# Three gate/up tiles leave the attention filler, the filler's order changes, and the sums of the input go to GpSimd

## The chip, the cores and the metric

The kernel runs on one core of one Trainium2 chip. The metric is device time in microseconds (us) of one execution, as the median of several runs; lower is better. The kernel before took 1116.48 us (median of 3, 1115.81 to 1116.67).

## The reference

One transformer block on x of 2048 tokens by 640, in float32. A layernorm without weights feeds two branches, and both are added to x:

```python
xn = _layernorm(x)                         # (x - mean) / sqrt(var + 1e-5)
# branch A: 32 heads of 20, causal, window of 256 tokens
q, k, v = split(xn @ wqkv)
scores = (q @ k^T) * 20 ** -0.5            # masked to 0 <= i - j < 256
o = softmax(scores) @ v
a = o @ wo                                 # 640 x 640
# branch B: gated MLP, 640 -> 1728 -> 640
g = xn @ w_gate ; u = xn @ w_up
b = (gelu_tanh(g) * u) @ w_down
out = x + a + b
```

## The kernel before

**Number format.** A dense product is made of three passes: each operand is split into a high and a low part of type fp32r, and high x high, low x high and high x low are added in PSUM (`dense_steps`, L78). With 640 = 5 x 128 inner rows, a 128 x 512 tile of output takes 15 matmuls, called steps here. The normalised input, transposed, stays in SBUF as `xh` and `xl`.

**Tiles of the MLP.** The 1728 columns of gate and up are 14 tiles f = 0 to 13 (the last one has 64 columns of each). A tile of gate and up for one of the four chunks of 512 tokens takes 2 x 15 = 30 steps, for all four chunks 120. The product gelu(g) * u is stored to DRAM (`hd`).

**Stages.** First a short stage does layernorm and transposes. Then comes attention (`attention`, L676), which takes more than half of the time. It runs over 32 units u (8 groups of 4 heads, times 4 chunks of tokens). Each unit is cut into NS = 14 slots, counted through the whole stage (slot 14u + i). The PE (TensorE) instructions of a unit are: matmuls for the maxima of the scores (`max_piece`, L410, 16 per unit, running one and a half units ahead), the scores again for the exponentials (`exp_piece`, L462, 12 per unit in three banks X, Y and Z, at slots 0 to 10), and in the next unit's first slot the product of P and v (`av_unit`, L484). DVE (VectorE) takes the maxima from PSUM (L412), ACT (ScalarE) the exponentials (L464), and POOL (GpSimd) zeroes the masked corners of P (`affine_select`, L470 and L473); `av_unit` needs all of a unit's selects.

**The filler.** Between these, `pull_fill` (L671) issues steps of dense work that attention does not need at once: RATE steps per unit, RATE / NS per slot. `filler` (L565) lists that work: q/k projections (`proj_qk`; q/k tile t of 10), v projections (`proj_v`), and gate/up tiles 0 to NFA - 1 and 13 (`gate_up_fill`, L520), in the order of the list `sets`. The second half of v is begun at the first turn after slot V1_SLOT. `gate_up_fill` makes the tanh form of gelu out of Square, Tanh and DVE operations (c1 to c5, each one slot after the other), since ACT also has to do Exp in this stage. A q/k projection is saved by `save_qk` (L196): ACT, DVE, ACT, and a subtraction on POOL (`pt`, L204), then stores on the SP queue. `load_stack` (L382) reads them back two units before they are used, six loads of 960 KB together.

**The seven-product phase.** After attention, tiles NFA to 12 are done by `gate_up_pair` (L833). It takes two chunks at once and uses seven block products in place of eight, over sums of weights (`w_sums`, on DVE) and sums of the input (`x_sums`, L602). A pair of chunks takes 54 matmuls, a tile 108, where the filler takes 120. Here gelu is one ACT operation. The sums of the input are made once, during attention: 8 groups (one per 50 slots from slot 24) of 10 operations on 128 x 256 elements, one per two slots, with four stores to DRAM (`td`, L616). They use two buffers `tx` in turn, so a new sum waits until the one two before has been stored.

**After that** the down projection and the output projection run (`terms`, L927), from 852 us to the end. The change touches nothing there.

**What sets the order.** In attention the orders on PE, ACT and DVE are written out by hand (`tc.manual_schedule(engines=MANUAL)`, with `defer` and `at` for slots). POOL and SP are not in that list: a planner puts their instructions into an order by times that it assumes, and each engine then executes its queue strictly in that order. The SP queue issues every DMA. In the seven-product phase SP is by hand too.

Of the kernel before, what the change touches and what calls it, by code (L numbers as in the profile page):

```python
# [12 lines left out]
AF = mybir.ActivationFunctionType  # L13
OP = mybir.AluOpType
# [10 lines left out]
NF = 14  # L25
# [2 lines left out]
NEG = -3.0e38  # L28
QROWS = 122
NS = 14  # L30
RATE = 49.6
V1_SLOT = 169
MXD = 4
NFA = 8
NDA = 2
WARM = 64
XS0, XSN = 24, 50
# [8 lines left out]
def block_kernel(ctx, tc, x, xt, wqk, wv, wo, wgu, wd, wdl, out):  # L46
    nc = tc.nc
# [30 lines left out]
    def dense_steps(ps, wh, wl, rh, rl, nk, cost=1.0):  # L78
        n = 0
        for a, b in ((wh, rh), (wl, rh), (wh, rl)):  # L80
            for k in range(nk):
                nc.tensor.matmul(ps, a(k), b(k), start=n == 0, stop=n == 3 * nk - 1)  # L82
                n += 1
                yield cost
# [89 lines left out]
    def defer(n, fn, *a):  # L174
        if now[0] is None:
            fn(*a)
        else:
            at(now[0] + n, fn, *a)
# [315 lines left out]
    def load_gu(f):  # L494
        raws = []
        for i in range(2 if f < NF - 1 else 1):
            raw = wrp.tile([128, KT, 128], F32, name="wr", tag="wr")
            nc.sync.dma_start(raw, wgu[2 * f + i])
            raws.append(raw)
        return raws  # L500
# [4 lines left out]
    def split_later(pool, bufs, raw):  # L505
        hi = pool.tile([128, KT, 128], F32R, name="wqh", tag="wqh", bufs=bufs)
        lo = pool.tile([128, KT, 128], F32R, name="wql", tag="wql", bufs=bufs)

        def high():
            nc.scalar.activation(hi, raw, AF.Copy)  # L510
            for k in range(KT):
                defer(1 + k, low, k)

        def low(k):
            nc.gpsimd.tensor_tensor(out=lo[:, k], in0=raw[:, k], in1=hi[:, k].bitcast(F32), op=OP.subtract)  # L515

        defer(1, high)
        return hi, lo

    def gate_up_fill(f, ws, c):  # L520
        cs = slice(c * C, (c + 1) * C)
        pss = []
        st = {}

        def c1():
            gs = st["g"] = hp.tile([128, C], F32, name="gs", tag="gs")
            t = st["t"] = hp.tile([128, C], F32, name="he", tag="he", bufs=2)
            nc.scalar.activation(gs, pss[0], AF.Copy)
            nc.scalar.activation(t, pss[0], AF.Square)
            defer(1, c2)  # L530

        def c2():
            gs, t = st["g"], st["t"]
            nc.vector.tensor_scalar(t, t, 0.044715, 1.0, op0=OP.mult, op1=OP.add)
            nc.vector.tensor_tensor(out=t, in0=gs, in1=t, op=OP.mult)
            defer(1, c3)

        def c3():
            nc.scalar.activation(st["t"], st["t"], AF.Tanh, scale=math.sqrt(2.0 / math.pi))
            defer(1, c4)  # L540

        def c4():
            nc.vector.scalar_tensor_tensor(st["g"], st["t"], 1.0, st["g"], op0=OP.add, op1=OP.mult)
            st["done"] = True

        def c5():
            if "done" not in st:
                defer(1, c5)
                return
            nc.vector.scalar_tensor_tensor(st["t"], st["g"], 0.5, pss[1], op0=OP.mult, op1=OP.mult)  # L550
            nc.sync.dma_start(hd[f][c], st["t"])

        for i, (wh, wl) in enumerate(ws):
            ps = psd.tile([128, C], F32, name="ps_d", tag="dn")
            pss.append(ps)
            yield from dense_steps(ps, lambda k: wh[:, k, :], lambda k: wl[:, k, :],
                                   lambda k: xh[:, k, cs], lambda k: xl[:, k, cs], KT)
            defer(1, c5 if i else c1)

    sets = [("qk", 1), ("gu", 0), ("qk", 2), ("gu", 1), ("qk", 3), ("gu", 2), ("qk", 4)]  # L560
    sets += [("gu", f) for f in range(3, NFA)] + [("gu", NF - 1)]
    pools = (wp, None), (hp, 2)
    rest = []

    def filler():  # L565
# [6 lines left out]
        for s, (kind, i) in enumerate(sets[:-1]):  # L572
            nxt = []
            after = sets[s + 1]
            for c in range(NC):
# [14 lines left out]
                if c in (1, 2) and c <= len(raws):  # L590
                    nxt.append(split_later(*pools[(s + 1) % 2], raws[c - 1]))
                if pending and now[0] >= V1_SLOT:
                    pending = False
# [8 lines left out]
    def x_sums(p, k, half):  # L602
        w = C // 2
        a, b = (slice((2 * p + i) * C + half * w, (2 * p + i) * C + half * w + w) for i in (0, 1))
        eh, el = xh.bitcast(F32), xl.bitcast(F32)
        live = {}

        def tile_of(i):
            live[i] = ap.tile([128, w], F32, name="tx", tag="tx")
            return live[i]  # L610

        def dve(o, i, j, op):
            nc.vector.tensor_tensor(out=o, in0=i, in1=j, op=op)

        def store(i):
            nc.sync.dma_start(td[p][i][:, k, half * w:half * w + w], live[i])  # L616

        def s1():
            dve(tile_of(1), eh[:, k, b], eh[:, k, a], OP.subtract)

        def s2():
            dve(live[1], live[1], el[:, k, b], OP.add)

        def s3():
            dve(live[1], live[1], el[:, k, a], OP.subtract)
            store(1)

        def s4():
            dve(tile_of(2), eh[:, k + 2, b], live[1], OP.subtract)

        def s5():
            dve(live[2], live[2], el[:, k + 2, b], OP.add)
            store(2)

        def s6():
            dve(tile_of(4), eh[:, k + 2, a], live[2], OP.subtract)

        def s7():
            dve(live[4], live[4], el[:, k + 2, a], OP.add)
            store(4)  # L640

        def s8():
            dve(tile_of(3), eh[:, k + 2, b], eh[:, k, b], OP.subtract)

        def s9():
            dve(live[3], live[3], el[:, k + 2, b], OP.add)

        def s10():
            dve(live[3], live[3], el[:, k, b], OP.subtract)
            store(3)  # L650

        return s1, s2, s3, s4, s5, s6, s7, s8, s9, s10

    NU = NG * NC
# [4 lines left out]
    def pull_max(n, slot):  # L659
        for _ in range(n):  # L660
            x = next(stream, None)
            if x is None:
                return
            max_piece(*x)
            if x[1] == 15:
                at(slot + MXD, max_end, x[0])
# [4 lines left out]
    def pull_fill(n):  # L671
        debt[0] += n
        while debt[0] > 0:
            debt[0] -= next(fill, 1.0)

    def attention():  # L676
# [15 lines left out]
        for u in range(NU + 1):  # L692
            if 1 <= u and u + 2 < NU:
                load_stack(u + 2)
            for i in range(NS):
# [5 lines left out]
                if i % 2 == 0:  # L701
# [3 lines left out]
                    pull_max(3 if i in (6, 12) else 2, T)  # L705
                pull_fill(RATE / NS)
        while acts:
# [77 lines left out]
    def load_xs(p, i):  # L785
        t = cp.tile([128, 2, C], F32, name="ht", tag="ht", bufs=3)
        nc.sync.dma_start(t, td[p][i])
        return t
# [167 lines left out]
    order.__enter__()  # L956
    raws_w = load_gu(NFA)
    xraw = {i: load_xs(0, i) for i in (2, 1, 3)}
# [61 lines left out]

    raws_next = {NFA + 1: load_gu(NFA + 1)}
    for j, f in enumerate(range(NFA, NF - 1)):
        end = f + 1 == NF - 1
# [56 lines left out]
    for n, (c, kind, i) in enumerate(steps):  # L1080
        if (kind, i) == ("d", 0):
            pss = [psn.tile([128, C], F32, name="ps_w", tag="w") for _ in range(KT)]
# [57 lines left out]
```

## Time and profile before

| | |
|---|---|
| median of 3 runs | 1116.48 us |
| profiled execution | 1116.69 us |
| its span in the profile | 1115.0 us |
| granted TensorE clock | 0.995 |
| busy share PE, DVE, ACT, POOL | 99%, 57%, 42%, 32% |

The profiled execution is 1.7 us longer than its span, and 0.2 us longer than the median. "Busy" for PE counts modelled ends of pipelined matmuls. A share of 99% thus says that little time is idle, not that each matmul is as short as it can be. The stages in the span: layernorm and start 0 to 92 us, attention 92 to 715 us, last gate/up tile 715 to 729 us, seven-product phase 729 to 852 us, down and output projection 852 to 1115 us.

### The profile page before, as it was taken

What the parts mean: (1) busy time and instruction counts of PE and PEld (TensorE: products, weight loads), DVE (VectorE), ACT (ScalarE), POOL (GpSimd) and SP (SyncE); (2) the same over time, 40 slices, a digit from 0 to 9 for tenths busy, and PEclk for the clock granted to TensorE, in tenths of its full rate; (3) what the DMA queues carried; (4) which work ended last, traced back from release to release, by engine and by line L of the source; (5) the groups of instructions that cost most, each with busy time, mean ns of one, the idle gap of its engine ahead of it and who ended that gap; (6) DMA issues with size and microseconds to landing.
All of it is one profiled execution on the core that took longest, in us unless ns stands there. A gap on an engine that the chain in (4) does not pass through costs nothing.

```text
span 1115.0 us, 19319 instructions
## 1 busy us (share of the span) xinstructions
PE 1098.7 (99%) x6802; PEld 837.6 (75%) x6802; DVE 637.7 (57%) x1736; ACT 470.9 (42%) x952; POOL 359.9 (32%) x504
## 2 busy tenths in 40 slices
PE   7999999999999999999999999999999999999998
PEld 7887666767668876667667676788888878788886
DVE  7856676757648577586777775566664350211203
ACT  4434554555555455645545454643323421211111
POOL 4122542644552233534323343311113313222230
PEclk8999999999999999999999999999999999999999
DMA  4642343543443314343242431342214835152431
GB/s 157 220 143 60 103 144 115 139 146 95 139 144 109 87 58 143 111 146 107 80 140 83 125 104 38 107 150 92 89 66 157 264 125 175 48 179 75 152 95 66
DMA packets 76145, 133.10 MB, mean 119 GB/s; under 512 B 12800, under 2 KB 33664, under 8 KB 76048
## 3 DMA queue, kind: packets, MB, share of 16 engines
q1 hardware_dynamic: 76048, 131.87, 37.6%
q8 instruction: 53, 0.87, 0.3%
q14 instruction: 44, 0.36, 0.1%
HBM read 86.31 MB, written 44.83 MB: 118 GB/s over the span
## 4 chain that ended last, share of the span: by engine, by line
PE 91%; DVE 4%; ACT 1%; DMA 1%; issue 1%; POOL 1%; SPq 0%; DVEq 0%; ACTq 0%; POOLq 0%
PE ps_d L82 28%; PE ps_w L942 23%; PE ps_g L851 11%; PE ps_o L484 7%; PE ps_e L462 7%; PE ps_m L410 6%; PE ps_v L82 6%; DVE junk L412 2%; PE ps_g L82 1%; PE ps_t L156 1%; PE ps_d L296 1%; ACT P L464 1%; PE ps_b L912 0%; DMA xi<-x 0%; DMA qs<-qd 0%
## 5 line engine op out<-in xcount | busy, mean ns | idle before, releaser
L412 DVE CUSTOM_DVE_ANT_0 junk<-ps_m,mask 128x384 bf16<-128x384 f32 (+2 forms) x512 | 271.2, 530 | 158.0 <-PE ps_m L410 120.0
L464 ACT ACTIVATE P<-ps_e 128x512 f32<-128x512 f32 (+2 forms) x384 | 197.5, 568 | 71.0 <-PE ps_e L462 64.6
L470 POOL TENSOR_SCALAR_AFFINE_SELECT P<-P 128x512 f32<-128x512 f32 x128 | 83.8, 655 | 221.1 <-ACT P L464 212.8
L82 PE MATMUL ps_d<-xh,wqh 128*128 128x512 f32 x510 | 150.4, 407 | 0.0
L82 PE MATMUL ps_d<-xh,wql 128*128 128x512 f32 x510 | 150.3, 407 | 0.0
L82 PE MATMUL ps_d<-xl,wqh 128*128 128x512 f32 x510 | 149.3, 406 | 0.0
L410 PE MATMUL ps_m<-ks,qs 120*128 120x128 bf16 (+1 forms) x704 | 120.9, 275 | 4.1 <-DVE mx L412 2.8
L921 POOL TENSOR_TENSOR ht<-hr,ht 128x512 fp32r<-128x512 f32 x52 | 69.2, 1337 | 172.1 <-ACT ht L919 142.9
L462 PE MATMUL ps_e<-qs,ks 122*128 122x128 bf16 (+2 forms) x704 | 112.5, 277 | 0.8 <-ACT P L464 0.6
L82 PEld LDWEIGHTS ps_d<-xl,wqh 128*128 128x128 f32 x510 | 92.9, 188 | 19.2 <-issue 2.4
L82 PEld LDWEIGHTS ps_d<-xh,wql 128*128 128x128 f32 x510 | 93.1, 189 | 18.0 <-issue 0.9
L82 PEld LDWEIGHTS ps_d<-xh,wqh 128*128 128x128 f32 x510 | 92.6, 188 | 17.2 <-ACT xh L164 0.3
L919 ACT ACTIVATE ht<-hr 128x512 fp32r<-128x512 f32 x56 | 35.1, 629 | 132.7 <-PE ps_w L942 80.8
L462 PEld LDWEIGHTS <-ks 122*128 122x128 bf16 x704 | 49.9, 98 | 54.6 <-issue 44.3
L473 POOL TENSOR_SCALAR_AFFINE_SELECT P<-P 128x512 f32<-128x512 f32 x112 | 74.2, 673 | 51.2 <-ACT P L464 51.2
L410 PEld LDWEIGHTS <-qs 120*128 120x128 bf16 x704 | 62.1, 98 | 33.1 <-issue 13.7
L484 PE MATMUL ps_o<-P,v 128*32 128x384 f32 (+2 forms) x1408 | 84.3, 386 | 0.0
L204 POOL TENSOR_TENSOR pt<-r,pt 128x512 bf16<-128x512 f32 x40 | 47.3, 1181 | 105.1 <-ACT pt L203 104.8
L484 PEld LDWEIGHTS ps_o<-P,v 128*32 128x32 f32 x1408 | 40.1, 110 | 39.6 <-issue 32.8
L923 DVE TENSOR_TENSOR ht<-hr,ht 64x512 fp32r<-64x512 f32 x4 | 2.8, 690 | 112.3 <-ACT ht L919 112.3
L515 POOL TENSOR_TENSOR wql<-wr,wqh 128x128 fp32r<-128x128 f32 x115 | 51.6, 481 | 38.0 <-ACT wqh L510 38.0
L488 ACT ACTIVATE ob<-ps_o 128x512 f32<-128x512 f32 x32 | 19.1, 597 | 101.1 <-PE ps_o L484 58.5
(270 smaller groups left out, 1889.2 us busy)
## 6 DMA issues: line engine op xcount, KB each, us to landing
hd<-he SPq DMA_DIRECT2D x52, 256.0 KB
hr<-hd SPq DMA_DIRECT2D x52, 256.0 KB
wr<-wgu SPq DMA_DIRECT2D x27, 320.0 KB
qs<-qd SPq DMA_DIRECT2D x32, 240.0 KB
ks<-kd SPq DMA_DIRECT2D x32, 240.0 KB
xi<-x SPq DMA_DIRECT2D x16, 320.0 KB
qs<-qd SPq DMA_DIRECT2D x32, 160.0 KB
ks<-kd SPq DMA_DIRECT2D x32, 160.0 KB
```

The lines of the kernel that those rows point to most:

```text
L82: nc.tensor.matmul(ps, a(k), b(k), start=n == 0, stop=n == 3 * nk - 1)
L410: nc.tensor.matmul(ps[:, lo:hi], lh, rhs, start=True, stop=True)
L412: nc.vector.tensor_tensor_reduce(out=junk[:, 0:n], in0=ps[:, 0:n], in1=mask[:, 384 - n:384], scale=1.0, scalar=NEG, op0=OP.add, op1=OP.max ...
L462: nc.tensor.matmul(ps[:, col:col + n], k[0:QROWS, j, kc:kc + 128], q[0:QROWS, j, q0:q0 + n], start=True, stop=True)
L464: nc.scalar.activation(pt[:, j, lo:hi], ps[:, lo:hi], AF.Exp, scale=SCALE)
L470: nc.gpsimd.affine_select(out=a, in_=a, pattern=[[0, 4], [1, 128]], compare_op=OP.is_ge, fill=0.0, base=0, channel_multiplier=-1)
L473: nc.gpsimd.affine_select(out=a, in_=a, pattern=[[0, 4], [-1, 128]], compare_op=OP.is_ge, fill=0.0, base=-1, channel_multiplier=1)
L484: nc.tensor.matmul(o[32 * j:32 * j + 32, q0:q0 + n], v[:, w0_:w0_ + 32], pt[:, j, col:col + n], start=i == 0, stop=i == len(todo) - 1, ski ...
L515: nc.gpsimd.tensor_tensor(out=lo[:, k], in0=raw[:, k], in1=hi[:, k].bitcast(F32), op=OP.subtract)
L851: nc.tensor.matmul(ps, i, j, start=first and n == 0, stop=n == len(work) - 1, skip_group_check=True)
L921: nc.gpsimd.tensor_tensor(out=t[:, 1, :], in0=raw, in1=t[:, 0, :].bitcast(F32), op=OP.subtract)
L942: nc.tensor.matmul(pss[m], w[:, ms], r, start=first and j == 0, stop=last and j == len(work) - 1)
```

## The change

- `NFA` goes from 8 to 5: tiles 5, 6 and 7 are no longer computed in the filler, but in the seven-product phase, which now has tiles 5 to 12 in place of 8 to 12.
- `RATE` goes from 49.6 to 38.4 steps per unit, so the smaller filler is spread over the same 32 units.
- `sets` is reordered: q/k tiles 1 and 2 first, then gate/up 0, q/k 3 and 4, then the other gate/up tiles.
- `V1_SLOT` goes from 169 to 174.
- The ten operations of each group of `x_sums` are issued on POOL in place of DVE. Their place on POOL's queue is up to the planner.
- In the filler's gelu, 0.044715 moves into the Square as a scale, and two DVE operations become one `scalar_tensor_tensor`.

```diff
-RATE = 49.6
-V1_SLOT = 169
+RATE = 38.4
+V1_SLOT = 174
...
-NFA = 8
+NFA = 5
...
-            nc.scalar.activation(t, pss[0], AF.Square)
+            nc.scalar.activation(t, pss[0], AF.Square, scale=math.sqrt(0.044715))
             defer(1, c2)
 
         def c2():
             gs, t = st["g"], st["t"]
-            nc.vector.tensor_scalar(t, t, 0.044715, 1.0, op0=OP.mult, op1=OP.add)
-            nc.vector.tensor_tensor(out=t, in0=gs, in1=t, op=OP.mult)
+            nc.vector.scalar_tensor_tensor(t, t, 1.0, gs, op0=OP.add, op1=OP.mult)
             defer(1, c3)
...
-    sets = [("qk", 1), ("gu", 0), ("qk", 2), ("gu", 1), ("qk", 3), ("gu", 2), ("qk", 4)]
-    sets += [("gu", f) for f in range(3, NFA)] + [("gu", NF - 1)]
+    sets = [("qk", 1), ("qk", 2), ("gu", 0), ("qk", 3), ("qk", 4)]
+    sets += [("gu", f) for f in range(1, NFA)] + [("gu", NF - 1)]
...
-        def dve(o, i, j, op):
-            nc.vector.tensor_tensor(out=o, in0=i, in1=j, op=op)
+        def pool(o, i, j, op):
+            nc.gpsimd.tensor_tensor(out=o, in0=i, in1=j, op=op)
...
         def s1():
-            dve(tile_of(1), eh[:, k, b], eh[:, k, a], OP.subtract)
+            pool(tile_of(1), eh[:, k, b], eh[:, k, a], OP.subtract)
...
```

The remaining lines of the diff replace `dve` by `pool` in s2 to s10 in the same way.

## The prediction

> **What bounds the kernel now.** First the page's busy shares, then the chain of work that ended last, then busy time by stretch.
>
> ```profile
> PE 1098.7 (99%) x6802; PEld 837.6 (75%) x6802; DVE 637.7 (57%) x1736; ACT 470.9 (42%) x952; POOL 359.9 (32%) x504
> ...
> PE 91%; DVE 4%; ACT 1%; DMA 1%; issue 1%; POOL 1%; SPq 0%; DVEq 0%; ACTq 0%; POOLq 0%
> PE ps_d L82 28%; PE ps_w L942 23%; PE ps_g L851 11%; PE ps_o L484 7%; PE ps_e L462 7%; PE ps_m L410 6%; PE ps_v L82 6%; DVE junk L412 2%; PE ps_g L82 1%; PE ps_t L156 1%; PE ps_d L296 1%; ACT P L464 1%; PE ps_b L912 0%; DMA xi<-x 0%; DMA qs<-qd 0%
> ```
>
> PE is the bound, and the chain is PE for 91%; the 2% of the maxima (L412) is where DVE is waited for. In the chain in order of time I read the attention units and the seven-product phase (start, length, count):
>
> ```profile
> 111.51 2.08 PE ps_o L484 x32
> 190.36 2.08 PE ps_o L484 x32
> 267.20 2.08 PE ps_o L484 x32
> 346.06 2.08 PE ps_o L484 x32
> 422.50 2.08 PE ps_o L484 x32
> 425.46 1.62 PE ps_d L82 x7
> 500.91 2.08 PE ps_o L484 x32
> 578.70 2.08 PE ps_o L484 x32
> 655.48 2.08 PE ps_o L484 x32
> 729.27 122.40 PE ps_g L851 x540
> ```
>
> Seven filler steps take 1.61 to 1.62 us: 0.230 us a step. The seven-product phase runs 540 matmuls without a break, 122.40 / 540 = 0.2267 us each. The x32 lines come once in four units: the fours last 78.85, 76.84, 78.86, 76.44, 78.41, 77.79 and 76.78 us, though PE's work differs little. Against the shortest, 8.9 us are lost to waits: mostly in fours with gelu and sums of the input together. By stretch (PE, PEld, DVE, ACT, POOL busy):
>
> ```profile
> 92.00:711.00 619.00, 614.09 (x4484) 438.28 (x4486) 419.20 (x1317) 328.23 (x674) 246.34 (x399) 1.00 0.36 110
> ...
> 778.23:802.71 24.48, 24.48 (x110) 20.27 (x109) 15.94 (x30) 7.07 (x15) 2.99 (x2) 1.00 0.23 79
> ```
>
> One tile of the seven-product phase takes 24.48 us with PE busy throughout, DVE at 65%. The groups that price the rest (mean ns of one):
>
> ```profile
> L921 POOL TENSOR_TENSOR ht<-hr,ht 128x512 fp32r<-128x512 f32 x52 | 69.2, 1337 | 172.1 <-ACT ht L919 142.9 <-DMA hr<-hd 29.1
> L515 POOL TENSOR_TENSOR wql<-wr,wqh 128x128 fp32r<-128x128 f32 x115 | 51.6, 481 | 38.0 <-ACT wqh L510 38.0
> L613 DVE TENSOR_TENSOR tx<-tx,xl 128x256 f32<-128x256 f32 x48 | 27.0, 564 | 0.0
> L535 DVE TENSOR_TENSOR he<-gs,he 128x512 f32<-128x512 f32 x32 | 24.0, 751 | 1.1
> L534 DVE TENSOR_SCALAR he<-he 128x512 f32<-128x512 f32 x32 | 14.7, 458 | 18.0 <-ACT he L529 17.8
> ```
>
> **The change part by part.**
>
> *Three tiles move.* The filler loses 3 x 120 = 360 steps x 0.230 = 82.9 us. The phase gains 3 x 24.48 = 73.4 us. Both are PE's path: **-9.5 us**. An added tile brings DVE 15.9, ACT 7.1 and POOL 3.0 us beside 24.48 us of PE; its two weight loads and eight stores lie in a DMA share of 0.23. All are hidden. Twelve filler gelus leave attention with their 1.8 us of ACT and 2.6 us of DVE each, as do 30 splits of 0.48 us on POOL: off the path by themselves.
>
> *Pace.* A unit loses 11.2 steps, 2.6 us: from 76.6 / 4 = 19.15 to some 16.55 us, a slot from 1.2 to 1.0 us. Attention's own work keeps its size, so every wait has less cover. DVE starts a maximum every 0.70 us in the timeline, 16 a unit: 11.2, and 0.3 for `nm`. Gelu then adds 14 slots / 11 per gelu = 1.28 x 3 operations of 0.7 = 2.7: 14.2 of 16.55, 86%. Before it was 15.8 of 19.15 (83%), and with sums (seven of 0.55 a unit where they run) 19.7, 103%. ACT's twelve exponentials at 0.55 us leave 0.9 us in each pair of slots of 2.0 us.
>
> *Sums off DVE, shorter gelu.* 80 sums (some 44 us) leave DVE, and L534 (0.46) goes from 20 gelus. The waits that this ends are in the 8.9 us: **-8.9**. What replaces them in gelu units is bounded by 0 (the four from 578.70, 0.3 us lost) and 0.6 us a unit (the worst fours, 2.4 us). I take 0.2, nearer the row at 83%, for 600 steps / 38.4 = 15.6 units: **+3.1** (0 to 9.4).
>
> *Sums on POOL.* No row has 256 columns there. Bounds are 0.48 (128 columns, L515) and 1.34 us (512, L921); between 0.48 and the 0.875 of the 320-column row (L239) it interpolates to 0.74, which I take. 80 x 0.74 = 59 us, less 14 for the splits, lift POOL from 40% to 53% of attention: not a bound. But POOL executes in order, and the planner's queue for the changed kernel puts the sums in clumps of up to five between the selects. Behind them stand the selects (`av_unit` waits), the q/k subtractions (L204), and on SP the stores of q/k with the loads of `load_stack` behind them. I follow POOL from a unit's start: selects of bank Y are ready at 10.1 and done at 12.0 us; those of Z are ready at 14.1, and PE wants Z at 16.6 + 1.8 = 18.4.
> Unit 7: five sums (3.7) and a weight split (2.4) stand between Y and Z: 18.1, and the first select ends at 18.7: 0.3 late.
> Unit 1: a split, a q/k subtraction (1.2) and four sums: 0.8 late.
> Unit 2: that lateness, one more sum and a subtraction end 4.4 us into it; three stores (1.3) and six loads (2.3 by the SP timeline) follow, and a load takes 3.88 us in the chain to land: 11.9, where the next stack's first maximum is due at 9.2: 2.7 late.
> Unit 11: v split, weight split and subtraction end 4.6 us into it: 2.9 late (before, that unit was already the longest, 20.43 us).
> Together **+6.7**; with sums of 0.48 or shorter waits it could be 0; with 1.34, 13.9.
> The `tx` stores now wait for POOL, but I find the maxima's rows (L427) queued behind them ready in time: with a slack of 1 us at units 11 and 13.
>
> *Order and V1_SLOT.* The q/k tiles now come with less filler work ahead of them. The second half of v starts at about slot 184 (the turn after V1_SLOT); at 9.75 / 2.74 = 3.6 slots per v tile its 16 tiles need 57 slots, and they are used over slots 238 to 294, the first four done by slot 198: hidden by some 40 slots of other work. Without that cover each late tile would cost its 9.75 steps, 2.2 us.
>
> Sum against the profiled execution: span 1115.0 - 9.5 - 8.9 + 3.1 + 6.7 = 1106.4, and 1.7 around it: **1108.1**; the median stands 0.2 below: **1108**.
>
> *A rule against it.* L613 has a median of 421 ns and a maximum of 1393, L535 starts 0.69 us apart when alone and has 1.00 beside POOL's work: DVE operations with both inputs in SBUF wait for POOL. The Trainium skill (SBUF - State Buffer, section Who interferes with whom) says that such an operation and a GpSimd instruction that reads SBUF take one port in turn, the second to issue blocking fully. The trace agrees; by that rule, two of gelu's three operations, blocked by a whole sum each, would make DVE's 14.2 us 16.1, just under 16.55, and by the rows' 0.2 to 0.3 us it is 15. The maxima (one input in PSUM) kept 0.56 us beside POOL's splits.
>
> **The rivals.**
> *A. Waits vanish.* The queues' slack is larger than I count (landing under 3.9 us): losses of 0 to 3 us, 1098.3 to 1101. For it: PE's recorded idle in attention is only 4.9 us.
> *B. The gain is eaten.* Sums of about 1.2 to 1.4 us (L921's length), or gelu units at 0.6 us: 1112 to 1117. Against it: L239 and L515 scale with columns.
> *C. Slower: POOL's sums delay the selects and stacks.* From 0.74 to 1.34 us the four places above lose 7.2 us more, 12 per us. The result is above 1118.7 once a sum takes 0.74 + 10.7 / 12 = 1.63 us, the length of 640 columns (L75, 1668 ns): 1119 to 1124. DVE's port waits speak for long sums, the 128-column row against.
> *D. DVE bounds gelu units.* By the port rule with waits on each gelu step: 16.1 to 17 us a unit, 0 to 0.5 us x 15.6: up to 1116. Against it: sums run in only 20 of 50 slots.
>
> **How the numbers follow.** Forecast 1102 to 1112: 0.57. A 0.13, B and D 0.18, C 0.12. A measurement tells 0.2% (2.2 us) from no change: faster is below 1114.2, slower above 1118.7. Faster: 0.57 + 0.13 + half of B and D = 0.79; same 0.09; slower 0.12. The bounds alone give 1098 to 1121; leaving out no more than 2 in 10, the range is 1101 to 1115.
>
> **What would show it.** The phase (L851) has 864 matmuls and about 196 us without a break; fours of units last about 66.5 us; L612 on POOL has 80 operations near 0.74 us; waits of L484 on POOL in units 1 and 7 and of L410 on loads in units 2 and 11. It is wrong if L484's waits on selects come in every unit, if L412 makes PE wait through whole gelu units, or if PE pauses between the phase's tiles.

## The result, and the profile after

The changed kernel takes **1126.05 us** (median of 4 runs, 1125.48 to 1126.12) beside 1116.58 us for the kernel before in the same session: a ratio of 1.0082 with a 95% interval of 1.0067 to 1.0097. It is slower by 0.8%, and 18 us above the 1108 us that were forecast. Its profiled execution took 1126.01 us with a span of 1124.3 us. All lines from L535 on have moved up by one against the kernel before.

The page's busy shares and its chain of work that ended last, by engine and by line:

```profile
PE 1097.3 (98%) x6766; PEld 832.2 (74%) x6766; DVE 610.0 (54%) x1657; ACT 467.6 (42%) x952; POOL 408.2 (36%) x560
...
PE 81%; DVE 6%; DMA 4%; issue 3%; ACT 3%; POOL 3%; SPq 1%; DVEq 0%; POOLq 0%; ACTq 0%
PE ps_w L941 19%; PE ps_d L82 18%; PE ps_g L850 17%; PE ps_o L484 7%; PE ps_m L410 6%; PE ps_e L462 5%; PE ps_v L82 5%; DVE junk L412 3%; DMA qs<-qd 2%; PE ps_g L82 1%; DMA od<-ob 1%; ACT P L464 1%; POOL ht L920 1%; PE ps_t L156 1%; POOL pt L204 1%
```

No engine but PE came near to being full: DVE fell from 57 to 54%, POOL rose from 32 to 36%. Yet PE's part of the chain went from 91 to 81%. Some of that is no loss: in the down and output projection the chain runs over PE for 222 of 264 us in place of 259 of 263, though PE waits for nothing there and the stage is as long as before, so there the chain only took another way. In attention PE's part went from 89% (552 of 623 us) to 74% (411 of 559 us), and what took its place is a bit of everything (DVE 46.5, DMA 33.2, ACT 26.0, POOL 19.1, "issue" 17.4 us). That is the picture of many short waits on several engines, and not of a new bound.

The chain in the order of time (start, length, count) says in which stage they lie:

```profile
110.06 2.17 PE ps_o L484 x32
182.10 2.08 PE ps_o L484 x32
251.22 2.08 PE ps_o L484 x32
326.16 2.16 PE ps_o L484 x32
394.38 2.08 PE ps_o L484 x32
463.35 2.08 PE ps_o L484 x32
531.50 2.08 PE ps_o L484 x32
...
650.88 13.89 PE ps_g L82 x60
664.78 195.85 PE ps_g L850 x864
```

The seven-product phase has its 864 matmuls in 195.85 us without a break, 73.45 us more than before, as forecast. From its end to the end of the span it is 263.7 us, against 263.3 before. So the error lies in attention: its last gate/up tile starts 64.5 us earlier than before (715.37 to 650.88), where the sum of the forecast wanted 82.0 (82.9 + 8.9 - 3.1 - 6.7). The fours of units last 72.0, 69.1, 74.9, 68.2, 69.0, 68.1 and 67.5 us, where about 66.5 were expected.

PE's waits in attention (90 to 651 us of the span; total, times, longest):

```profile
PE ps_m L410 <- DMA od<-ob: 6.1, 5, 2.5
PE ps_m L410 <- DVE mx L412: 5.6, 18, 0.4
PE ps_e L462 <- ACT P L464: 2.1, 5, 0.6
```

The first line is the loads of `load_stack`: the matmuls of L410 read only `ks` and `qs`, which these loads fill, and the profile puts the end of the wait down to a store (`od<-ob`) on the same queue. These 13.8 us were 4.3 us before (2.8 for maxima, 0.9 for transfers, 0.6 for exponentials). They are less than what was lost. One reason is that a wait is counted only from the modelled end of the last matmul: a filler step is recorded with 0.39 us, and the next one starts 0.23 us after it, so a stop is recorded some 0.16 us short. I therefore use another measure from here on: a unit's length less 0.2303 us for each filler step in it, the one that reaches over its start included (a 320-column step counted as 0.64 of one). What is left is the unit's own work. Unit n is here the stretch from the nth start of value products to the next. What is left is at its shortest about 7.33 us in one half of the units and 7.65 us in the other half, whose score matmuls are cut differently (7.31 and 7.63 in the kernel before, 7.35 and 7.78 in the changed one). What lies above 7.33 or 7.65 us, the same two figures in every run, I call the unit's **loss**. Summed over units 1 to 28, and split by what the changed kernel's filler mainly holds there:

```
loss, us              1-5   6-9   10-13  14-17  18-20  21-28   all
                      q/k   g/u   q/k    v      q/k    g/u
before                2.4   0.6    2.0   0.3    1.9    1.3     8.6
changed               6.0   3.5    8.9   2.0    2.6    3.2    26.1
forecast for changed                                           9.8
```

In the kernel before, q/k and gate/up work are mixed from unit 1 on, so its row stands for the same units and not for the same work. Two thirds of the changed kernel's loss, 17.5 of 26.1 us, lie in units whose filler is nearly all q/k work, with hardly a gelu. The forecast had charged the shorter pace to gelu's units alone.

### The profile page after: what moved, and what is told of

It reads as the page before. It is cut to its first block, busy times and chain, and to the rows that moved or that the text cites. A ratio compares the mean times of both kernels' runs of the same rounds, so it can differ in the third digit from the quotient of the medians.

```text
span 1124.3 us, 19237 instructions
## 1 busy us (share of the span) xinstructions
PE 1097.3 (98%) x6766; PEld 832.2 (74%) x6766; DVE 610.0 (54%) x1657; ACT 467.6 (42%) x952; POOL 408.2 (36%) x560
## 4 chain that ended last, share of the span: by engine, by line
PE 81%; DVE 6%; DMA 4%; issue 3%; ACT 3%; POOL 3%; SPq 1%; DVEq 0%; POOLq 0%; ACTq 0%
PE ps_w L941 19%; PE ps_d L82 18%; PE ps_g L850 17%; PE ps_o L484 7%; PE ps_m L410 6%; PE ps_e L462 5%; PE ps_v L82 5%; DVE junk L412 3%; DMA qs<-qd 2%; PE ps_g L82 1%; DMA od<-ob 1%; ACT P L464 1%; POOL ht L920 1%; PE ps_t L156 1%; POOL pt L204 1%
## 5 line engine op out<-in xcount | busy, mean ns | idle before, releaser
L412 DVE CUSTOM_DVE_ANT_0 junk<-ps_m,mask 128x384 bf16<-128x384 f32 (+2 forms) x512 | 271.8, 531 | 170.9 <-PE ps_m L410 128.4
L470 POOL TENSOR_SCALAR_AFFINE_SELECT P<-P 128x512 f32<-128x512 f32 x128 | 83.6, 653 | 176.6 <-ACT P L464 171.9
L410 PE MATMUL ps_m<-ks,qs 120*128 120x128 bf16 (+1 forms) x704 | 122.8, 275 | 11.9 <-DMA od<-ob 6.1
L920 POOL TENSOR_TENSOR ht<-hr,ht 128x512 fp32r<-128x512 f32 x52 | 69.1, 1333 | 172.6 <-ACT ht L918 152.7
L82 PE MATMUL ps_d<-xh,wqh 128*128 128x512 f32 x390 | 119.2, 412 | 0.0
L82 PE MATMUL ps_d<-xh,wql 128*128 128x512 f32 x390 | 118.8, 413 | 0.0
L82 PE MATMUL ps_d<-xl,wqh 128*128 128x512 f32 x390 | 118.4, 412 | 0.0
L462 PE MATMUL ps_e<-qs,ks 122*128 122x128 bf16 (+2 forms) x704 | 114.8, 278 | 3.3 <-ACT P L464 2.1
L410 PEld LDWEIGHTS <-qs 120*128 120x128 bf16 x704 | 61.9, 98 | 44.0 <-issue 20.7
L473 POOL TENSOR_SCALAR_AFFINE_SELECT P<-P 128x512 f32<-128x512 f32 x112 | 71.7, 651 | 26.5 <-ACT P L464 26.5
L82 PEld LDWEIGHTS ps_d<-xl,wqh 128*128 128x128 f32 x390 | 71.2, 190 | 13.6 <-issue 0.9
L82 PEld LDWEIGHTS ps_d<-xh,wql 128*128 128x128 f32 x390 | 70.8, 189 | 13.2 <-issue 1.1
L204 POOL TENSOR_TENSOR pt<-r,pt 128x512 bf16<-128x512 f32 x40 | 46.5, 1163 | 93.2 <-ACT pt L203 90.4
L82 PEld LDWEIGHTS ps_d<-xh,wqh 128*128 128x128 f32 x390 | 70.2, 189 | 13.2 <-issue 0.8
L75 POOL TENSOR_TENSOR wql<-wr,wqh 128x640 fp32r<-128x640 f32 x12 | 19.5, 1626 | 157.5 <-PE ps_g L850 127.6
L484 PEld LDWEIGHTS ps_o<-P,v 128*32 128x32 f32 x1408 | 40.1, 110 | 39.4 <-issue 28.4
L488 ACT ACTIVATE ob<-ps_o 128x512 f32<-128x512 f32 x32 | 19.1, 597 | 108.6 <-issue 60.0
```

What stands on the lines that cost most here:

```text
L204: nc.gpsimd.tensor_tensor(out=pt[:, l, :], in0=r, in1=pt[:, 1, :], op=OP.subtract)
L410: nc.tensor.matmul(ps[:, lo:hi], lh, rhs, start=True, stop=True)
L412: nc.vector.tensor_tensor_reduce(out=junk[:, 0:n], in0=ps[:, 0:n], in1=mask[:, 384 - n:384], scale=1.0, scalar=NEG, op0=OP.add, op1=OP.max ...
L462: nc.tensor.matmul(ps[:, col:col + n], k[0:QROWS, j, kc:kc + 128], q[0:QROWS, j, q0:q0 + n], start=True, stop=True)
L470: nc.gpsimd.affine_select(out=a, in_=a, pattern=[[0, 4], [1, 128]], compare_op=OP.is_ge, fill=0.0, base=0, channel_multiplier=-1)
L473: nc.gpsimd.affine_select(out=a, in_=a, pattern=[[0, 4], [-1, 128]], compare_op=OP.is_ge, fill=0.0, base=-1, channel_multiplier=1)
```

## The experiments

Two theories stood at first. The **queue theory** says that the sums on POOL delay selects, q/k subtractions and loads more than I counted. The **pace theory** says that units 2.6 us shorter no longer cover waits that attention has anyway, wherever the sums are. A third came later.

### Sums back on DVE; sums on POOL alone; order alone; pace alone

The first is the changed kernel with one line undone, the others are the kernel before with one part of the change done.

```diff
 # sums back on DVE (changed kernel)
-            nc.gpsimd.tensor_tensor(out=o, in0=i, in1=j, op=op)
+            nc.vector.tensor_tensor(out=o, in0=i, in1=j, op=op)
 # sums on POOL alone (kernel before)
-            nc.vector.tensor_tensor(out=o, in0=i, in1=j, op=op)
+            nc.gpsimd.tensor_tensor(out=o, in0=i, in1=j, op=op)
 # order alone (kernel before)
-V1_SLOT = 169
+V1_SLOT = 174
-    sets = [("qk", 1), ("gu", 0), ("qk", 2), ("gu", 1), ("qk", 3), ("gu", 2), ("qk", 4)]
-    sets += [("gu", f) for f in range(3, NFA)] + [("gu", NF - 1)]
+    sets = [("qk", 1), ("qk", 2), ("gu", 0), ("qk", 3), ("qk", 4)]
+    sets += [("gu", f) for f in range(1, NFA)] + [("gu", NF - 1)]
 # pace: order alone, and the rate; the filler's last 360 steps run after attention
-RATE = 49.6
+RATE = 38.4
```

> The changed kernel with the sums of the input back on VectorE; all else stays (five tiles in the filler, 38.4 steps per unit, new order, short gelu). Queue theory (the sums on GpSimd delay the selects, the q/k subtractions and so the loads of the stacks): those delays go, the 15 us that the forecast missed go with them, about 1108 to 1114 us. Pace theory (a unit that is 2.6 us shorter no longer covers the latencies of attention's own loads, maxima and exponentials, whoever makes the sums): VectorE carries 44 us more in the same short units, 1125 to 1133 us.

> The kernel before with only the sums of the input moved to GpSimd (eight tiles in the filler, 49.6 steps per unit, old order and gelu). Queue theory: the late selects and loads come here too, 1119 to 1126 us. Pace theory: units of 19.2 us cover the sums on GpSimd, and VectorE's waits in the units with sums go: 1110 to 1116 us.

> The kernel before with only the new order of the filler (q/k tiles 1 and 2, gate/up 0, q/k 3 and 4, then the rest) and V1_SLOT 174, at the old 49.6 steps per unit. Both theories: the order moves no bound, 1115 to 1119 us. A third, that the order itself costs (q/k and value work bunched in the first half, where each saved projection puts stores ahead of the loads): 1121 to 1126 us.

> The kernel before with the new order and V1_SLOT 174 and with 38.4 steps per unit, but all eight tiles still in the filler and the sums on VectorE: the 360 steps that do not fit are issued after attention. The work is that of the kernel before, only attention's units are 2.6 us shorter. Pace theory: attention waits as in the changed kernel, 15 to 25 us more than before, 1130 to 1142 us. Queue theory: the pace costs a few us at most, 1116 to 1122 us.

| kernel | median, us | ratio to before (95%) | loss, us |
|---|---|---|---|
| changed, sums on DVE | 1130.47 | 1.0122 (1.0101 to 1.0144) | 31.7 |
| before, sums on POOL | 1117.85 | 1.0006 (0.9996 to 1.0016) | 10.4 |
| before, new order | 1115.53 | 0.9995 (0.9985 to 1.0005) | 7.0 |
| the same at the new pace | 1143.98 | 1.0242 (1.0222 to 1.0263) | 32.9 |

The last two differ in the rate alone. The steps left over run after attention at the same 0.23 us, so no work is added, and still the time grows by 28.4 us and the loss by 25.9 us. The order costs nothing. Moving the sums costs nothing clear of noise at the old pace, but gains nothing either. At the new pace it gains 4.4 us (1130.47 to 1126.05). So the pace theory holds in the main, and the sums on POOL are a help and not the culprit.

### GpSimd's order by hand; no sums at all

```diff
-    with tc.manual_schedule(engines=MANUAL):
+    with tc.manual_schedule(engines=MANUAL | {mybir.EngineType.Pool}):
```

> The changed kernel with GpSimd's order in attention written by hand as the program issues it, instead of the planner's order with its clumps of sums; all else, the sums on GpSimd among it, stays. Queue theory (the clumps of sums ahead of selects and q/k subtractions, about 7 us in units 1, 2, 7 and 11, are much of the 18 us that went missing): 1117 to 1121 us, and unit 11 falls from 20.9 us to 18 or less. Pace theory (units of 16.6 us do not cover the waits of attention itself): 1123 to 1128 us, whatever unit 11 does; the maxima's waits stay near 5 us.

```diff
-            live[i] = ap.tile([128, w], F32, name="tx", tag="tx")
+            live[i] = eh[:, k, b]
...
-            nc.gpsimd.tensor_tensor(out=o, in0=i, in1=j, op=op)
+            pass
```

> The changed kernel with the sums of the input left out: GpSimd's 80 subtractions and additions are gone, and the stores write the high half of the input in their place, so that all transfers stay (the four sums are then not the reference's, and the time is that of the kernel without them). It measures all that the sums cost where the change put them. Queue theory: 1126 - 7 to 10 = 1116 to 1119 us, with units 1, 2, 7 and 11 at 16.6 to 17.5 us. Pace theory: units of 16.6 us wait for other things, 1121 to 1125 us, with the waits for maxima still there.

By hand it is 1122.88 us, a ratio of 1.0052 (1.0037 to 1.0067); the loss of units 10 to 13 falls from 8.9 to 5.5 us, and unit 11 from 20.9 to 17.9 us. Without sums it is 1123.47 us (1.0061, 1.0046 to 1.0076). Each is some 3 us below the changed kernel. In the second run the stores write the high half of the input in place of the sums, so that all transfers stay. The queue theory is therefore true and small: all that the sums cost where they were put is 2.6 us, give or take 2 us by the intervals. The late load of unit 11 is there without any sums too, with a stop of 3.00 us. The sums themselves were sized well. The changed kernel's sums (line, engine, times; ns least, median, most):

```profile
L612 POOL TENSOR_TENSOR tx<-tx,xl x48: 722/732/1198, 67.2 to 565.6; 128x256 f32<-128x256 f32 x48
```

### Maxima and exponentials in smaller bursts; no gelu

```diff
 # one maximum per slot
-                    pull_max(3 if i in (6, 12) else 2, T)      # every second slot
+                pull_max(2 if i in (6, 12) else 1, T)          # every slot
 # both per slot
-                        exp_piece(u, i)                        # every second slot
-                        exp_piece(u, i + 1)
+                    exp_piece(u, i)                            # every slot
```

> The changed kernel with the sixteen maxima of a unit handed out one to a slot (two at slots 6 and 12) instead of two or three to every second slot. What PE waits for in the pace theory is partly the burst: two or three maxima of 0.70 us on VectorE in a pair of slots that now lasts 2.4 us with gelu operations between. If the burst is the cause, VectorE's waits (5.6 us recorded, more behind them) go and the time is 1112 to 1121 us; if the mean load or other latencies are the cause, 1124 to 1128 us. The queue theory expects no change: 1126 us.

> As the run with the maxima spread, and the twelve exponentials of a unit also one to a slot instead of two to every second slot. If exponentials in pairs (two banks, 0.55 us each on ScalarE behind gelu's activations) add to the waits, 1 to 4 us less than with the maxima spread alone: 1110 to 1119 us; if not, the same as that run. The queue theory expects 1126 us.

One maximum per slot gives 1121.27 us (1.0045, 1.0028 to 1.0062), both per slot 1123.50 us (1.0058, 1.0035 to 1.0080). The bursts of maxima are thus worth some 5 us; spreading the exponentials as well gives none of it more, and its profiled execution has two late loads (3.49 and 4.35 us, in units 2 and 11) that hide what it might: the other seven of units 1 to 5 and 10 to 13 lose 4.5 us in it, where they lose 8.4 us in the changed kernel. Neither takes the loss of the q/k units away as a whole: units 1 to 5 and 10 to 13 still hold 14.3 of 22.5 us in the first, where unit 11 also holds a late load.

The filler's gelu was then left out: `c2` to `c4` and the Square are gone, and `c5` multiplies up by half of gate.

```diff
-            nc.scalar.activation(t, pss[0], AF.Square, scale=math.sqrt(0.044715))
-            defer(1, c2)
...
-            nc.scalar.activation(st["t"], st["t"], AF.Tanh, scale=math.sqrt(2.0 / math.pi))
...
```

> The changed kernel with the filler's gelu left out (up is multiplied by half of gate in its place): two of three VectorE operations and two of three ScalarE operations of each of the 24 filler gelus are gone, 48 x 0.7 us on VectorE and 48 x 0.55 us on ScalarE. Its output is not the reference's. Pace theory in the form that the maxima and exponentials wait behind gelu: 1126 - 6 to 10 = 1116 to 1120 us, and VectorE's waits fall below 2 us. In the form that each slot of 1.2 us is too short for the attention's own chain (score matmul, maximum or exponential, free buffer) whatever stands beside it, and in the queue theory: 1123 to 1126 us.

It takes 1121.67 us (1.0044, 1.0032 to 1.0056). The loss of the gate/up units falls (6 to 9 from 3.5 to 1.9, 21 to 28 from 3.2 to 1.3), that of the q/k units does not: 20.2 us in place of 17.5, with a late load in unit 2. (The profiled execution, 1125.08 us, is the longest of nine.) So gelu's work in its units, the only ones that I had charged, is worth about 3.5 us of the 26.

### Six and seven tiles in the filler

```diff
-RATE = 38.4
+RATE = 45.9     # seven tiles; 42.1 for six
...
-NFA = 5
+NFA = 7         # or 6
```

> The changed kernel with 7 gate/up tiles in the filler instead of 5 (so one of the three stays moved) at a rate of 45.9 steps a unit; sums stay on GpSimd, gelu short. Without any waits two tiles moved back cost 2 x (240 / 2 x 0.2303 - 24.48) = 6.3 us. Pace theory: the missing 18 us shrink with the longer units (18.3 us instead of 16.6) to 5 to 8 us, and the time is 1126 + 6.3 - 10 to 13 = 1119 to 1122 us or less. If the loss came only from the clumps of GpSimd's queue or from the move itself, whatever the pace, the time would be 1130 to 1133 us.

> Seven tiles in the filler (1110.7 us with the planner's order) with GpSimd's order written by hand as well. Queue theory: the hand order takes the 3 us that it took at five tiles, 1107 to 1109 us. Pace theory: at units of 18.3 us the clumps have cover, 0 to 1.5 us, 1109 to 1111 us.

> Six tiles in the filler at 42.1 steps a unit, GpSimd's order by hand: the point between 1122.9 us (five tiles, by hand) and the run with seven. Pace theory: the waits grow faster than the tile's 3.2 us gain, so the time lies between, 1112 to 1118 us, with a loss against full cover of 9 to 13 us. If the loss were a fixed one of the move to five tiles (that tile's place, the order of q/k), six tiles would be 3 us faster than seven: 1104 to 1108 us.

| tiles in the filler | GpSimd's order | median, us | ratio to before (95%) | loss, us |
|---|---|---|---|---|
| 7 | planner | 1110.74 | 0.9944 (0.9930 to 0.9959) | 7.0 |
| 7 | by hand | 1111.08 | 0.9950 (0.9935 to 0.9965) | 7.0 |
| 6 | by hand | 1113.47 | 0.9969 (0.9957 to 0.9981) | 11.9 |
| 5 | by hand | 1122.88 | 1.0052 (1.0037 to 1.0067) | 23.7 |
| 5 | planner | 1126.05 | 1.0082 (1.0067 to 1.0097) | 26.1 |

With one tile moved instead of three, the same change is **faster** than the kernel before by 0.56%, and lies 8 us below the 1119 us that the pace theory named (with "or less" added), and further below the other theory's range. From seven to five tiles (by hand) a unit loses 7.5 steps, 1.7 us, and the loss of all units goes from 7.0 to 23.7 us, where the two tiles bring 6.3 us. By hand and by planner are the same at seven tiles: so at that pace POOL's clumps cost nothing that can be measured.

### What the q/k units wait for: the hand-over

Unit 10 of the changed kernel (268.4 to 287.1 us) has no gelu, its sums come only in its last 4 us, and it loses 2.1 us. PE's timeline (start, length, instruction, idle before it) shows it stop twice for a free exponential bank; this is the first stop:

```profile
273.10 0.61 PE L462 MATMUL ps_e<-qs,ks 122*128 122x128 bf16 x4
...
275.75 0.86 PE L462 MATMUL ps_e<-qs,ks 122*128 122x128 bf16 x4 [0.55 <-ACT P L464]
```

ACT's timeline at that place:

```profile
273.14 0.61 ACT L215 ACTIVATE pt<-ps_d 128x512 bf16<-128x512 f32 x1
274.58 0.63 ACT L203 ACTIVATE pt<-r 128x512 bf16<-128x512 f32 x1 [0.83 <-DVE r L216]
275.11 2.22 ACT L464 ACTIVATE P<-ps_e 128x512 f32<-128x512 f32 x4
```

And DVE's:

```profile
273.85 0.69 DVE L216 TENSOR_TENSOR r<-ps_d,pt 128x512 f32<-128x512 f32 x1 [0.61 <-ACT pt L215]
274.46 0.55 DVE L412 CUSTOM_DVE_ANT_0 junk<-ps_m,mask 128x384 bf16<-128x384 f32 x1
```

Read them together. `save_qk` hands a tile from ACT (first copy, L215) to DVE (subtraction, L216) and back to ACT (second copy, L203). The subtraction is issued in the same slot as the copy, so DVE stands 0.61 us for it, with two maxima behind. The second copy is issued one slot later, so ACT stands 0.83 us for the subtraction. Behind it are the exponentials of the two banks that PE filled at 273.1 us, and PE then stands 0.55 us for the bank that the first of them frees. Two engines that are 54% and 42% busy stop PE, because each executes in order. The Trainium skill (Perfetto Trace Analysis, section Tensor Engine Instruction (MATMUL, LD_WEIGHTS)) states just that: ACT, DVE and GPSIMD take their queues strictly first in, first out. The lines above agree with it.

The wait was there before. In the kernel before, in attention:

```profile
ACT pt L203 <- DVE r L216: 16.8, 18, 2.0
```

The runs with the new order show what the pace does to its price: at the old rate ACT stands 17.3 us in 20 stops at L203, and units 1 to 5, 10 to 13 and 18 to 20 lose 3.6 us; at the new rate it stands 18.5 us in 22 stops, and they lose 18.0 us. One slot was 1.37 us then (19.2 / 14) and is 1.18 us now (16.55 / 14). This third theory was tested by giving the hand-over more slots, and nothing else (the planner then orders POOL and SP anew):

```diff
         def upper():
             nc.scalar.activation(pt[:, h, :], ps, AF.Copy)
+            defer(1, middle)
+
+        def middle():
             nc.vector.tensor_tensor(out=r, in0=ps, in1=pt[:, h, :], op=OP.subtract)
-            defer(1, lower)
+            defer(2, lower)
```

> The changed kernel with longer hand-overs in the filler's q/k work: VectorE's subtraction one slot after ScalarE's copy (instead of in the same slot) and ScalarE's second copy two slots after that (instead of one). Hand-over theory (in-order engines stand at these operations with exponentials and maxima queued behind): units 3 to 4, 10, 12, 13 fall by 0.5 to 1.5 us each, 1126 - 4 to 9 = 1117 to 1122 us. If the unit's length or the engines' load is the cause: 1125 to 1127 us. Against it: later q/k tiles may make the loads of units 2 and 11 up to 3 us later each.

> As the run with longer hand-overs in q/k work, and the filler's gelu with two slots instead of one between VectorE's product and ScalarE's tanh. Hand-over theory: 1 to 4 us less than that run (units 7, 8, 9, 22 to 27, which lost 0.3 to 1.3 us each). Else the same within 1 us.

With the longer hand-over it takes 1114.83 us (0.9978, 0.9969 to 0.9987): **11.2 us less** than the changed kernel, at five tiles and the full pace, and no longer slower than the kernel before. ACT's waits for the subtraction in attention, in the changed kernel:

```profile
ACT pt L203 <- DVE r L216: 15.7, 22, 1.4
```

and with the longer hand-over:

```profile
ACT pt L203 <- DVE r L219: 3.3, 7, 0.8
```

DVE's stops for the first copy fell with them, from 9.7 to 2.3 us.

ACT's timeline at the same place of unit 10 now has two exponentials ahead of the copy and no stop before it:

```profile
271.87 0.61 ACT L215 ACTIVATE pt<-ps_d 128x512 bf16<-128x512 f32 x1
272.34 1.11 ACT L467 ACTIVATE P<-ps_e 128x512 f32<-128x512 f32 x2
273.30 0.67 ACT L203 ACTIVATE pt<-r 128x512 bf16<-128x512 f32 x1
```

```
loss, us              1-5   6-9   10-13  14-17  18-20  21-28   all
changed               6.0   3.5    8.9   2.0    2.6    3.2    26.1
longer hand-over      1.5   2.7    2.4   2.0    0.9    2.9    12.4
```

The q/k units lose 4.8 us in place of 17.5; the late loads of units 2 and 11 are nearly gone with it (one recorded stop of 0.2 us in unit 11), though the sums are still on POOL in the planner's order. That part of the gain, 5.9 of the 13.7 us by which the loss fell, has another path than ACT's stop. The SP queue at unit 11 of the changed kernel, which begins at 287.13 us, and then at unit 11 with the longer hand-over, from 283.94 us:

```profile
290.53 1.30 SPq L210 DMA_DIRECT2D kd<-pt  x3
291.93 1.15 SPq L390 DMA_DIRECT2D qs<-qd  x3
```

```profile
286.39 1.13 SPq L393 DMA_DIRECT2D qs<-qd  x3
292.31 1.67 SPq L210 DMA_DIRECT2D kd<-pt  x3
```

In the changed kernel the three stores of a q/k tile stand ahead of the loads, which start 4.8 us into the unit. With the longer hand-over the tile is ready later, its stores go behind the loads, and these start 2.5 us into the unit. In unit 2 they start 0.4 us in place of 4.9 us into it. The other q/k units, where no load stops PE, lose 4.3 us in place of 11.0. Two delays were changed at once here, so which of the two stops mattered more was not told apart, and neither were the two paths by a run.

The same medicine for gelu's tanh (`defer(2, c3)`), for which ACT also waits, 11.5 us in 12 stops in the changed kernel, takes these stops from 11.1 to 1.8 us and gains nothing: 1115.47 us (0.9985, 0.9975 to 0.9994). A wait of nearly the same size on the same engine is covered there. The size of a wait on ACT alone does not tell its price.

### The hand-over's own cost, and the best versions

> Six tiles in the filler, GpSimd's order by hand, both longer hand-overs (1113.5 us without them). Hand-over theory: 3 to 6 us less, 1107 to 1110 us, below the run with seven tiles. If not: 1112 to 1115 us.

> Seven tiles, GpSimd's order by hand, both longer hand-overs (1111.1 us without them). At this pace little is left to wait for: the units stand some 5 us above their shortest, so 1107 to 1111 us by the hand-over theory, 1110 to 1112 us without.

Neither expectation held: the runs took 1116.93 us at six tiles (0.9997, 0.9987 to 1.0006) and 1113.46 us at seven (0.9969, 0.9955 to 0.9983), 3.5 and 2.4 us above the same kernels with the short hand-overs. Attention's loss did fall by 1.4 us in each, but the first unit's value products start at 114.3 and 116.6 us in place of 108.9 and 110.6. The run at five tiles had this too (113.9 us against 110.0). In that run PE's waits before 118 us of the span have two new lines:

```profile
PE ps_v L82 <- DVE r L219: 2.7, 2, 1.9
PE ps_v L82 <- DVE v L272: 1.2, 1, 1.2
```

Before the first unit, filler steps are issued more densely per slot (`RAMP`, `GAP`), and a subtraction one slot later holds one of the two `ps_d` banks that the next tile needs. So the last two runs keep the short hand-over before slot 4 of the first unit:

```diff
+            if now[0] is None or now[0] < 4:
+                middle(1)
+            else:
+                defer(1, middle, 2)
```

> The changed kernel with the longer hand-overs of q/k work from slot 4 of the first unit on, and the short ones before it. Hand-over theory: the 4 us at the start come back, attention keeps its units of 16.3 to 18 us: 1110 to 1112 us, below the kernel before by 0.4 to 0.6%. If the later start has another cause, 1114 to 1116 us.

> The same with six tiles in the filler, GpSimd's order the planner's. One tile less moved costs 3.2 us without waits; the excess of units 7, 8, 12, 16 and 22 to 25 (some 7 us at five tiles) should fall by half: 1109 to 1112 us, within 2 us of the run with five tiles. If waits do not shrink with the pace once the hand-overs are mended: 1113 to 1115 us.

Five tiles: **1111.71 us** (0.9953, 0.9941 to 0.9966), 14.3 us below the changed kernel by this edit alone; the first unit starts at 109.6 us. Six tiles: **1110.41 us** (0.9937, 0.9923 to 0.9950). That and the seven tiles with the short hand-over (1110.74 us) both beat the kernel before and the changed one by clear intervals, and are the same to each other.

## Why the prediction was wrong, step by step

- **Three tiles move (-9.5 us): right.** The phase grew by 73.45 us against 73.4. Units without loss are as long as their steps say: the shortest, unit 21, is 16.33 us with 39 steps (one of them reaching over its start), which leaves 7.35 us, as before (7.31).
- **Waits that end when the sums leave DVE and gelu is shortened (-8.9 us): wrong.** I took all that the long fours lose for the work of sums and gelu. At the old pace the sums' move alone brought nothing (1.0006, 0.9996 to 1.0016). Its loss is 1.8 us higher than that of the kernel before: 2.6 us more in units 10 to 13, 0.8 us less in all others. The forecast looked at fours, in which q/k, gelu and sums overlap, and gave their loss to the work that the change removes. The shorter gelu was not run alone. It can hardly have brought much: with sums on DVE at the new pace, the changed kernel with the short gelu loses 31.7 us, and the kernel with the long one and all eight tiles 32.9.
- **New waits from the shorter pace (+3.1 us, bounds 0 to 9.4): the step that failed.** It charged 0.2 us to gelu's 15.6 units and nothing to the q/k units, with no reason given for that. For gelu's units the price was about right (3.5 us by the run without gelu); the q/k units lose 17.5 us. The pace alone costs 25.9 us of loss with the sums still on DVE, and the changed kernel's loss is 26.1 where the forecast's terms left 9.8 in all. The reasoning was by load: "ACT's twelve exponentials at 0.55 us leave 0.9 us in each pair of slots". The slots were too short there (1.2 and 1.0 us, where 19.15 / 14 and 16.55 / 14 are 1.37 and 1.18 us), so the room is 1.3 us and larger than I said, and it did not help. ACT's stops at L203 (16.8 us, mostly covered at the old pace) were in the trace of before, and I didn't ask what is queued behind them. Lengthening the hand-over took 13.7 us off the loss, 5.9 us of it by way of the loads of units 2 and 11, and 14.3 us off the time with the start mended.
- **Sums on POOL (+6.7 us): duration right, price high.** 0.73 us each against 0.74. The stops at the loads of units 2 and 11 came as forecast (1.93 and 2.46 us against 2.7 and 2.9), but that of unit 11 stays without any sums (3.00 us), the longer hand-over brought such stops down to 0.2 us in its first run and 2.8 us in the run with the start mended, with the sums still on POOL, and all sums together cost 2.6 us. PE's stop in unit 7 was for maxima; its waits for selects are 0.4 us or less each.
- **Order and V1_SLOT (nothing): right**, 0.9995 (0.9985 to 1.0005).
- **Rivals.** The sign was that of C and the time lay above its 1119 to 1124 us, but not its mechanism: it needed sums of 1.63 us. D (DVE bounds gelu's units by the shared port) showed nothing of its size: gelu's first product (L534) has a median of 690 ns, and leaving most of gelu out saves some 4 us by the median. The three signs that would show it wrong (selects in every unit, L412 through whole gelu units, pauses in the seven-product phase) were also not those that came.

What stays open: 12.4 to 14.2 us of loss remain at five tiles with the hand-over mended, 4.4 to 5.2 us of it recorded as waits for maxima. The run with maxima spread says that the bursts are part of it; the two edits were not run together.

## What to carry to other kernels

Before the units of such a schedule are made shorter, list the stops of the engines that are *not* the bound, and for each what is queued behind it: at a longer period these stops can be covered and free, and the busy shares here did not say at which period they surface. Delays that are counted in slots of a schedule shrink with the slot, while the operations that they were to cover do not, so such delays have to be set anew with the pace, and only where a bank stands free to hold the result meanwhile. And a gain per moved unit of work can be right and still not add up: here the kernel with one tile moved gained 0.56%, and the third tile cost 9.4 us by hand order (1113.47 to 1122.88), about as much as all three were to bring.

## What the hardware showed that was not expected

The stop of 2.46 us in unit 11 cost more than itself. PE's timeline, and then the table by stretch of the changed kernel (after each stretch: length, busy time of PE, PEld, DVE, ACT and POOL, granted TensorE clock, DMA share, GB/s):

```profile
298.95 0.33 PE L410 MATMUL ps_m<-ks,qs 120*128 120x128 bf16 x2 [2.46 <-DMA od<-ob]
```

```profile
298.00:300.00 2.00, 1.05 (x5) 0.89 (x6) 0.95 (x3) 0.00 (x0) 0.94 (x2) 0.78 0.49 146
300.00:302.00 2.00, 2.00 (x7) 1.23 (x6) 0.00 (x0) 0.00 (x0) 0.00 (x0) 0.50 0.36 109
302.00:304.00 2.00, 2.00 (x12) 1.43 (x10) 0.95 (x3) 1.59 (x4) 0.00 (x0) 0.86 0.01 4
```

The granted clock drops to 0.50. What is missing from full clock in these three stretches (0.22, 0.50 and 0.14 of 2 us each) is 1.7 us, some 3.4 us at half clock, and that is lost on top of the stop. Over all twenty profiled executions, ten stops of PE in attention's units were 1.90 us or longer: with six the clock fell to half (1.90, 2.46, 2.89, 3.36, 3.49 and 4.35 us), twice for some 6.8 us and else for 3.4 us; with four it did not (1.93, 2.31, 2.53 and 3.00 us), and of seven stops of 1.26 to 1.69 us it did with none. So it is not the length alone that decides. In the run without gelu the stop of 2.89 us made unit 2 22.83 us long, 3.8 us longer than in the changed kernel. The Trainium skill (TensorE: Matmul & The Clock Gate, section What's actually happening) says that the clock falls to half after at least one idle window of about 3.4 us, and that these windows run freely. Windows that do not start with the stop fit that stops of like length go either way; that a stop recorded with 1.90 us (some 0.16 us short, as said) was enough does not fit the full window that the page asks for, and there the measurement stands. A late load that stops PE for 2 us or more is thus to be priced with the clock that may follow.
